# q and some softmax sums turned by VectorE in 32x32 blocks, in a fused attention and channel-mix kernel

## The chip, the cores and the metric

The kernel runs on one core of one Trainium2 chip. The core has engines that work side by side, each through its own instructions in order: TensorE (PE, with its weight loads as PEld), VectorE (DVE), ScalarE (ACT), GpSimd (POOL) and SyncE (SP); POOL and SP mostly issue DMAs here. The metric is the device time in microseconds of one execution; lower is better. A measured time is a median of several executions. A profile is one further execution with its own time.

## The reference

Inputs are fp32: q, k, v of shape 8 x 8 x 576 x 64 (batch, head, token, head dimension), phi of 8 x 8 x 576 x 32, and the weights of a channel mix. The work per batch and head is an attention with 32 memory slots in place of keys:

```python
a = phi - np.max(phi, axis=2, keepdims=True)
a = np.exp(a)
a = a / (np.sum(a, axis=2, keepdims=True) + 1e-09)      # over tokens
k_m = np.einsum('bhsm,bhsd->bhmd', a, k)
v_m = np.einsum('bhsm,bhsd->bhmd', a, v)
scores = scale * np.matmul(q, k_m.transpose(0, 1, 3, 2))
attn = np.exp(scores - np.max(scores, axis=-1, keepdims=True))
attn = attn / (np.sum(attn, axis=-1, keepdims=True) + 1e-09)   # over the 32 slots
x = np.matmul(attn, v_m)          # then heads side by side: 8 x 576 x 512
x_prev = x shifted by one token, zero at each batch's start
xk = mu_k * x + (1.0 - mu_k) * x_prev
xr = mu_r * x + (1.0 - mu_r) * x_prev
k = np.maximum(xk @ w_k, 0.0)     # 512 -> 1024
v = k * k @ w_v                   # 1024 -> 512
r = 1.0 / (1.0 + np.exp(-(xr @ w_r)))
out = r * v
```

Neither maximum is taken on the chip.

## The kernel before

**Layout.** A batch's 8 heads form HH = 4 pairs; g is the pair and c (0 or 1) the head in it. Where slots lie on partitions, pair g has the 32 partitions from 32 g on, for each c. q, k and v come in as bf16 with 128 partitions, where a partition holds a run of NJ = 9 tokens for each pair; rows 0 to 63 belong to c = 0, rows 64 to 127 to c = 1 (ROWS). A batch's tokens are worked in two column halves of 320 and 256 (HALVES).

**Steps of a batch.** PLAN (L18 to L38) is an order written out by hand: a list of words, run from left to right, each issuing a step's instructions to their engines. So it fixes the order on every engine and every queue. A word "3:l2" is step l2 of batch 3. The steps are: exp (exponential of phi, L225), z (sum over tokens as matmuls, and reciprocal, L247 to L250), kv or k, v (k_m and v_m, L237), nk and nv (scaled by the reciprocal, L274, L281), tk (k_m turned by TensorE and copied to kmT, L301 to L305), q0 and q1 (q turned), s0 and s1 (scores and their exponentials e, L358 to L362), l0 to l3 (denominators: a matmul with ones sums the 32 slots and spreads the sum, then a logarithm, L372 to L377), r0z and r1z (exponential of minus the logarithm, L382), w0 and w1 (e times that, at, L389), x0 and x1 (times v_m, to PSUM, copied by ScalarE, L288 to L401), dd (difference to the token before, L413), and k0d, k2d, r0d, r2d (the two mixes, L423 to L424, written to rings xk_T and xr_T). Batches 0 and 1 take a shorter way for the mixes: nk0 to nr1, y0 to y3 and mk0 to mr1 (mixed, L437) put mu into v_m and mix in PSUM. A suffix c, hn, ht, h0z or qh marks a step on half a batch.

**Steps of the channel mix.** "c3:5" is key step 5 of token chunk 3 (512 tokens; chunk 0 in two halves a and b): 4 matmuls, relu on ScalarE (rl, three buffers), square on VectorE (sq, L520 to L528). "g:7" is the gate of 128 tokens: 4 matmuls, exponential (L548), and for odd ones a logarithm and exponential over the pair (L550, L551). "o:7" is the value: 8 matmuls, a product with the gate on VectorE and the store (L565 to L567; L505 for the DMA on SP). "p:..." words and "load" issue loads on POOL's queue ("2:load" loads batch 4; LOADS, L40, gives the order phi, k, v, q, and k, q, v for batch 2). "0:busy4" puts four matmuls of zeros on TensorE. "0:mub" and "0:mu" prepare mu.

**How q is turned.** The scores need q with the head dimension on partitions. Batch 0 (qh0, qh1; L319) and batches 1 to 4 (q0, q1; L333) do it on TensorE: matmuls with the identity to PSUM, then copies by VectorE (and ScalarE for batches 0 and 1). Batches 5 to 7 (qx, L314) use a DMA that turns, issued from SP; "5:hold" (L263) is a tiny POOL copy that makes POOL's queue wait for batch 5's turned q before "5:load" overwrites q. Two tokens' 64 elements share one turned block of 128 rows, so that even and odd token runs j lie in different row halves; for that reason JT (L46) puts the nine runs in the order 0 2 4 6 8 1 3 5 7, and the store (L504) undoes it.

**Shared buffers.** All matmul outputs go through one pool of 8 PSUM banks, handed out in the order of PLAN; scores' two halves are matmuls on tiles of 64 rows x 32 columns of the array, written as

```python
for g in (0, 2, 1, 3):
    m = slice(g * M, (g + 1) * M)
    for hf in range(2):
        n = [NJ * g + j for j in JT[5 * hf:5 + 4 * hf]]
        r = ROWS[n[0] % 2]
        nc.tensor.matmul(pss[hf][m, :], lhsT=st["kmT"][r, c, m], ...)
```

Of the kernel before, what the change touches and what calls it, by code (L numbers as in the profile page):

```python
# [10 lines left out]
F32 = mybir.dt.float32  # L11
BF16 = mybir.dt.bfloat16
AF = mybir.ActivationFunctionType
# [5 lines left out]
    "p:q:0a 0:exp1 0:exp0 0:z 0:k0c p:q:0b 0:hn0 0:qh0 0:ht0 0:qh1 p:k:0b 0:s0 0:mub p:v:0a 0:l0 0:k1c 0:l1 0:hn1",  # L19
    "p:v:0b 0:mu 0:ht1 p:wr:0-4 0:h1z 0:v0c 0:s1 0:v1c p:phi:1 0:h0z 0:y1 0:l2 0:l3 0:nk0 0:y0 0:nk1 0:h3z 0:nr1",  # L20
    "p:wk:4-8 0:h2z 0:busy4 0:nr0 0:y3 0:y2 0:mr1 0:mr0 p:wk:0-4 0:mk1 1:exp g:2 g:0 0:mk0 g:3 1:z c0:2a c0:7b c0:6b",
    "c0:4a c0:1b p:k:1 p:q:1 c0:2b 1:k 1:nk c0:0b c0:7a c0:5b c0:3a c0:1a 1:q0 c0:3b 1:q1 1:tk c0:4b c0:0a 1:s0 p:v:1",
    "1:s1 1:v c0:6a 1:l1 1:nr1 1:l0 c0:5a p:wv:0-2 1:nk0 1:l2 p:wv:2-4 1:nk1 1:nr0 1:h1z 1:l3 0:load 1:y1 1:h2z 1:h0z",
    "1:h3z g:1 1:y3 o:3a o:2a 1:y2 1:y0 o:2b o:3b 1:mk1 o:1b 1:mk0 1:mr0 c1:5 1:mr1 c1:2 2:exp c1:6 c1:3 c1:1 c1:0",
    "1:load 2:z g:4 g:5 2:q1 2:q0 2:kv 2:nk o:0b 2:load o:1a 2:tk 3:exp 2:nv c1:7 2:s1 2:s0 c1:4 2:l2 o:0a 2:l1 3:z",
    "2:l0 2:r0z 2:w0 2:l3 2:r1z 2:w1 o:4 o:5 2:x0 3:kv 3:nk 3:nv g:6 3:tk 3:q0 3:q1 2:x1 2:dd 2:k0d g:7 g:8 3:s0",
    "2:k2d 3:s1 o:6 o:7 3:l0 2:r2d 3:l2 3:load 3:l1 2:r0d 3:l3 3:r1z c2:3 4:exp c2:2 c2:5 3:r0z 3:w1 c2:0 3:w0 c2:4",
    "c2:6 g:10 c2:1 4:z 3:x1 4:kv 4:nk 4:nv c2:7 3:x0 g:11 3:dd 4:q0 4:q1 4:tk 5:exp o:11 g:9 5:qx o:10 5:z 5:kv",
    "3:k0d 4:s1 3:k2d 4:s0 o:9 g:12 4:l3 5:nk 3:r0d 4:l2 c3:2 c3:6 5:nv 4:l0 4:l1 4:r1z 4:w1 c3:3 4:r0z 4:w0 5:tk",
    "c3:7 c3:4 3:r2d c3:0 c3:5 5:s0 5:hold 5:load 4:x1 o:8 c3:1 5:l1 4:x0 4:dd g:13 4:k2d 5:l0 g:14 o:13 4:load o:12",  # L30
# [14 lines left out]
NJ = 9  # L45
JT = (0, 2, 4, 6, 8, 1, 3, 5, 7)  # L46
# [3 lines left out]
def kernel(  # L50
# [23 lines left out]
    QR = S // NJ  # L74
    HALVES = (slice(0, 5 * QR), slice(5 * QR, S))
# [135 lines left out]
    def attention(b):  # L211
# [51 lines left out]
        def hold():  # L263

            spare = work.tile([1, 2], BF16, name="spare", tag="spare", bufs=1)
            nc.gpsimd.tensor_copy(spare, st["qT"][0:1, :, 0, 0])

        def norm_k(cs=(0, 1)):

            def go():  # L270
                if "kbd" not in st:
                    st["kbd"] = work.tile([128, 2, 2, D], BF16, name="kbd", tag="kbd", bufs=3)
                for c in cs:
                    nc.vector.tensor_scalar_mul(  # L274
                        st["kbd"][:, c], st["k"][c].unsqueeze(1).to_broadcast([128, 2, D]), st["rz"][:, c:c + 1])
            return go
# [30 lines left out]

        def q_tile():
            if "qT" not in st:
                st["qT"] = work.tile([128, 2, HH * NJ // 2, QR], BF16, name="qT", tag="qT", bufs=3)  # L310
            return st["qT"]

        def cross_q():
            for hg in range(2):  # L314
                nc.sync.dma_start_transpose(out=q_tile()[:, hg],
                                            in_=qs[b % 2][ROWS[hg]].rearrange("p n d -> p (n d)"))

        def tr_q_rows(hg):

            def go():  # L320
                r = ROWS[hg]
                for i in range(2):
                    ps = ps_tile([128, NJ, QR], BF16, "qtps")
                    for n in range(NJ):
                        n0 = 2 * (NJ * i + n)
                        nc.tensor.matmul(ps[:, n], rhs=identity[r, r], is_transpose=True,  # L326
                                         lhsT=qs[b % 2][r, n0:n0 + 2, :].rearrange("p n d -> p (n d)"),
                                         start=True, stop=True, skip_group_check=True)
                    (nc.scalar.copy if i else nc.vector.tensor_copy)(q_tile()[:, hg, NJ * i:NJ * (i + 1)], ps)
            return go  # L330

        def tr_q(i):
            def go():  # L333
                pss = [ps_tile([128, NJ, QR], BF16, "qtps") for _ in range(2)]
                for n in range(NJ):
                    n0 = 2 * (NJ * i + n)
                    for hg in range(2):
                        r = ROWS[hg]
                        nc.tensor.matmul(pss[hg][:, n], rhs=identity[r, r], is_transpose=True,  # L339
                                         lhsT=qs[b % 2][r, n0:n0 + 2, :].rearrange("p n d -> p (n d)"),  # L340
                                         start=True, stop=True, skip_group_check=True)
                for hg in range(2):
                    (nc.scalar.copy if b < 2 and hg else nc.vector.tensor_copy)(
                        q_tile()[:, hg, NJ * i:NJ * (i + 1)], pss[hg])
            return go

        def scores(c):

            def go():
                if "e" not in st:  # L350
                    st["e"] = work.tile([128, 2, S], BF16, name="e", tag="e", bufs=3)
                pss = [half_tile(hf, "scps") for hf in range(2)]
                for g in (0, 2, 1, 3):
                    m = slice(g * M, (g + 1) * M)
                    for hf in range(2):
                        n = [NJ * g + j for j in JT[5 * hf:5 + 4 * hf]]
                        r = ROWS[n[0] % 2]
                        nc.tensor.matmul(pss[hf][m, :], lhsT=st["kmT"][r, c, m],  # L358
                                         rhs=st["qT"][r, c, n[0] // 2:n[-1] // 2 + 1].rearrange("p j t -> p (j t)"),
                                         start=True, stop=True, skip_group_check=True)  # L360
                for hf in range(2):
                    nc.scalar.activation(st["e"][:, c, HALVES[hf]], pss[hf], AF.Exp, scale=scale)  # L362
            return go
# [20 lines left out]

        def weigh(c, sl=slice(0, S)):
# [51 lines left out]
        def mixed(w, hf):  # L437

            def go():
# [7 lines left out]
                for i in range(ND):  # L447
# [27 lines left out]
        for i in range(2):  # L475
            steps[f"s{i}"] = scores(i)
# [19 lines left out]
    def store(o, t, cols):  # L496
        g = t * 128
        eng = nc.sync
        while g < (t + 1) * 128:
# [4 lines left out]
            dst = out[b].rearrange("(p j) d -> p j d", j=NJ)[p0:p0 + n, JT[j], cols]  # L504
# [32 lines left out]
    def gate(t):  # L537

        def go():
# [5 lines left out]
            if t % 2 == 0:  # L545
# [3 lines left out]
            if t % 2 == 1:  # L549
# [71 lines left out]
```

## Time and profile before

| what | value |
|---|---|
| time, median of 3 runs | 208.34 us (207.24 to 208.76) |
| the profiled execution | 208.79 us, its span 207.0 us |
| TensorE busy | 192.7 us (93%) |
| VectorE busy | 133.9 us (65%) |
| ScalarE busy | 159.4 us (77%) |
| GpSimd busy | 29.6 us (14%) |
| mean TensorE clock granted | 0.998 |
| HBM read, written | 38.28 MB, 9.44 MB |

The span runs from the first to the last instruction; the execution's own time lies a little over it. Busy time of TensorE counts pipelined matmuls with modelled ends, so that rows of matmuls overlap, and where one block ends is read better from the start of the next. A row of the groups gives line, engine, operation, output and inputs with shapes, count, then busy time and mean ns of one, then the idle time before them and what ended it. A row of the view of waits reads: who waited, for whom, us in total, times, longest. Lengths of neighbouring VectorE rows overlap by some hundredths of a microsecond.

### The profile page before, as it was taken

Reading aid. Unit: us, or ns where it says so; the run is one execution under the profiler, and the core shown is the slowest. Engines: PE = TensorE matmul, PEld = TensorE weight load, DVE = VectorE, ACT = ScalarE, POOL = GpSimd, SP = SyncE. Lnnn points to the kernel's source line nnn. Section 1 sums busy time; section 2 is a strip of 40 time slices with the busy share of each in tenths; the row PEclk is TensorE's granted clock in tenths of the full one; section 3 lists DMA queues with packets and bytes.
Section 4 is the critical chain, followed back from the end, with each engine's and each line's share of the span. In section 5 each row is a group of like instructions: output and inputs, shape, how many; then the busy total and the mean of one; then the engine's idle time right before and its main releaser. Section 6 shows DMA issues by size and latency. Waiting matters only on the chain.

```text
span 207.0 us, 5511 instructions
## 1 busy us (share of the span) xinstructions
PE 192.7 (93%) x2213; PEld 103.6 (50%) x2235; DVE 133.9 (65%) x360; ACT 159.4 (77%) x314; POOL 29.6 (14%) x46
## 2 busy tenths in 40 slices
PE   0489999999999999999999999999999999999992
PEld 0355577745655445544458654444444444444441
DVE  1236455884668996899594969767887856615232
ACT  3246999987968998979899977899968655686570
POOL 7644222201504000007400000000000000000000
PEclk9999999999999999999999999999999999999999
DMA  6999999999999999298999997832060215202525
GB/s 160 178 208 260 207 207 205 261 221 292 209 284 240 262 269 201 61 133 205 187 231 298 198 165 115 189 71 52 0 152 5 51 33 119 54 0 62 135 67 141
DMA packets 31641, 33.06 MB, mean 160 GB/s; under 512 B 9072, under 2 KB 26752, under 8 KB 31616
## 3 DMA queue, kind: packets, MB, share of 16 engines
q0 software_dynamic: 17392, 20.91, 54.2%
q1 hardware_dynamic: 13456, 10.96, 24.5%
q10 hardware_dynamic: 768, 0.85, 1.3%
q8 instruction: 17, 0.28, 0.5%
q14 instruction: 8, 0.07, 0.1%
HBM read 38.28 MB, written 9.44 MB: 231 GB/s over the span
## 4 chain that ended last, share of the span: by engine, by line
PE 89%; DMA 6%; issue 1%; POOL 1%; ACT 1%; DVE 0%; SPq 0%; POOLq 0%; DVEq 0%
PE pk L520 31%; PE pv L565 29%; PE pr L543 15%; DMA q<-in_q_dram 4%; PE kvps L237 3%; PE zps L372 2%; PE mxps L288 2%; DMA qT<-q 2%; PE scps L358 2%; PE nops L288 2%; PE qtps L339 1%; PE idle L195 1%; PE zps L247 1%; PE mub L200 1%; PE qtps L326 1%
## 5 line engine op out<-in xcount | busy, mean ns | idle before, releaser
L520 PE MATMUL pk<-xkT,wk 128*128 128x512 bf16 (+4 forms) x346 | 66.9, 340 | 0.4
L565 PE MATMUL pv<-wv,sq 128*128 128x512 bf16 (+1 forms) x322 | 65.6, 353 | 0.4
L524 ACT ACTIVATE rl<-pk 128x512 bf16<-128x512 f32 (+3 forms) x80 | 41.9, 560 | 9.9 <-PE pk L520 8.7
L528 DVE TENSOR_TENSOR sq<-rl 128x512 bf16<-128x512 bf16 (+5 forms) x104 | 32.3, 340 | 26.0 <-ACT rl L524 25.0
L565 PEld LDWEIGHTS <-sq 128*128 128x128 bf16 x328 | 31.4, 98 | 30.0 <-issue 0.5
L520 PEld LDWEIGHTS <-wk 128*128 128x128 bf16 x352 | 32.9, 98 | 26.5 <-issue 0.5
L567 DVE TENSOR_TENSOR o<-sg,pv 128x512 f32<-128x512 f32 (+1 forms) x41 | 24.9, 619 | 18.9 <-PE pv L565 14.1
L543 PE MATMUL pr<-wr,xrT 128*128 128x512 bf16 x134 | 34.6, 381 | 0.5
L548 ACT ACTIVATE sg<-pr 128x512 f32<-128x512 f32 x36 | 21.3, 611 | 12.3 <-PE pr L543 5.2
L543 PEld LDWEIGHTS <-xrT 128*128 128x128 bf16 x144 | 13.5, 98 | 15.4 <-ACT xrT L449 0.4
L550 ACT ACTIVATE sg<-sg 128x1024 f32<-128x1024 f32 x18 | 19.0, 1057 | 0.6
L551 ACT ACTIVATE sg<-sg 128x1024 f32<-128x1024 f32 x18 | 19.0, 1057 | 0.6
L401 ACT CAST x<-nops 128x320 bf16<-128x320 f32 (+1 forms) x48 | 15.8, 428 | 3.6 <-PE nops L288 3.6
L423 DVE TENSOR_SCALAR mu_d<-diff,mu 128x576 bf16<-128x576 bf16 x48 | 15.5, 364 | 0.1
L389 DVE TENSOR_TENSOR atn<-e,lz 128x576 bf16<-128x576 bf16 (+2 forms) x20 | 12.4, 635 | 4.0 <-ACT lz L382 3.8
L377 ACT ACTIVATE lz<-zps 128x320 f32<-128x320 f32 (+1 forms) x32 | 11.9, 420 | 1.6 <-PE zps L372 1.6
L362 ACT ACTIVATE e<-scps 128x320 bf16<-128x320 f32 (+1 forms) x32 | 11.0, 416 | 1.5 <-PE scps L358 1.5
L382 ACT ACTIVATE lz<-lz 128x576 f32<-128x576 f32 (+2 forms) x20 | 11.6, 600 | 0.2
L413 DVE TENSOR_TENSOR diff<-x 128x1024 bf16<-128x1024 bf16 (+1 forms) x18 | 9.0, 554 | 3.4 <-ACT x L401 3.4
L225 ACT ACTIVATE em<-ph 128x1152 bf16<-128x1152 f32 (+1 forms) x9 | 9.4, 1050 | 2.1 <-DMA ph<-in_phi_dram 2.1
L237 PE MATMUL kvps<-kv,em 64*32 64x128 bf16 (+1 forms) x720 | 9.3, 219 | 1.0 <-DMA kv<-in_k_dram 1.0
L424 DVE TENSOR_TENSOR xkT<-x,mu_d 128x1152 bf16<-128x1152 bf16 x12 | 9.1, 759 | 0.4
(66 smaller groups left out, 140.7 us busy)
## 6 DMA issues: line engine op xcount, KB each, us to landing
out_dram<-o SPq DMA_DIRECT2D x61, 128.0 KB, 2.4
ph<-in_phi_dram POOLq DMA_DIRECT2D x7, 576.0 KB, 20.8
kv<-in_k_dram POOLq DMA_DIRECT2D x7, 576.0 KB, 17.3
q<-in_q_dram POOLq DMA_DIRECT2D x7, 576.0 KB, 21.3
kv<-in_v_dram POOLq DMA_DIRECT2D x7, 576.0 KB, 18.8
out_dram<-o SPq DMA_DIRECT2D x18, 64.0 KB, 5.6
wk<-in_moe_w_k_dram POOLq DMA_DIRECT2D x2, 512.0 KB, 14.7
wv<-in_moe_w_v_dram POOLq DMA_DIRECT2D x2, 512.0 KB, 20.0
```

Source lines behind the costliest of these rows:

```text
L237: nc.tensor.matmul(kvps[c][g * M:(g + 1) * M], lhsT=em[ROWS[c], j, g, :], rhs=kv5[ROWS[c], parts, g, j, :], start=j == 0, stop=j == NJ - 1 ...
L401: nc.scalar.copy(st["x"][:, i, sl], pss[i])
L423: nc.vector.tensor_scalar_mul(t[:, i], st["d"][:, pr + i, :], mu1[:, o:o + 1])
L520: nc.tensor.matmul(pk[:, p0 - lo:p1 - lo], lhsT=wk_sb[:, di, fi * 128:(fi + 1) * 128], rhs=xk_T[:, di, p0 % RING:p0 % RING + p1 - p0], sta ...
L524: nc.scalar.activation(rl, pk, AF.Relu)
L528: nc.vector.tensor_mul(sq[:, fi, p:p + p1 - p0], rl[:, p0 - lo:p1 - lo], rl[:, p0 - lo:p1 - lo])
L543: nc.tensor.matmul(pr, lhsT=xr_T[:, di, c0:c0 + 128], rhs=wr_sb[:, di, :], start=(di == 0), stop=(di == ND - 1))
L548: nc.scalar.activation(sg[:, t % 2], pr, AF.Exp, scale=-1.0)
L550: nc.scalar.activation(sg, sg, AF.Ln, bias=1.0)
L551: nc.scalar.activation(sg, sg, AF.Exp, scale=-1.0)
L565: nc.tensor.matmul(pv[:, cols], lhsT=sq[:, fi, p:p + 128], rhs=wv_sb[:, fi, cols], start=(fi == 0), stop=(fi == NF - 1))
L567: nc.vector.tensor_mul(o[:, cols], gated[t // 2][:, t % 2, cols], pv[:, cols])
```

## The change

q is turned by VectorE for all batches. VectorE's turn works on 32x32 blocks of 32-bit words; the bf16 data are read as words, so that a word holds two neighbouring elements of the head dimension and stays whole. The steps q0 and q1 now issue one VectorE instruction each (128 partitions, 576 words); qh0 and qh1 of batch 0 turn 64 partitions with 1152 words. TensorE's and the DMA's turning, their PSUM copies, JT, qx and hold go away. qT has two buffers in place of three.

After the turn a partition quadrant holds, for one c and one half of the token rows, 32 words of the head dimension, and the two elements of each word lie side by side (index h). So a score is the sum of two matmuls over 32 rows each (h = 0 and 1), with kmT split the same way (norm_k writes even and odd elements apart, and repeats them for the two token halves). Scores use tiles of 32 x 32, with the moving operand read at every second element; step "s" does both c of a batch at once in four PSUM banks, while batch 0 keeps s0 and s1. The exponentials write e with tokens in their natural order, and the differences, mixes and stores use that order.

For batches 5 to 7 the denominators no longer go through TensorE and ScalarE. "fe" turns e in 32x32 word blocks, "fs" sums over the 32 slots along the free axis and takes the reciprocal, and "fo" spreads that over 32 and turns it back into lz. These replace l0 to l3 and r0z, r1z there.

The gate's logarithm and second exponential are a step of their own ("sg:3" for the pair 3). PLAN is written anew, loads included: weights come as wk's lower half, wr, wk's upper half; batch 2 loads in the common order.

```diff
 PLAN = [
-    "p:q:0a 0:exp1 0:exp0 0:z 0:k0c p:q:0b 0:hn0 0:qh0 0:ht0 0:qh1 p:k:0b 0:s0 0:mub p:v:0a 0:l0 0:k1c 0:l1 0:hn1",
-    "p:v:0b 0:mu 0:ht1 p:wr:0-4 0:h1z 0:v0c 0:s1 0:v1c p:phi:1 0:h0z 0:y1 0:l2 0:l3 0:nk0 0:y0 0:nk1 0:h3z 0:nr1",
-    "p:wk:4-8 0:h2z 0:busy4 0:nr0 0:y3 0:y2 0:mr1 0:mr0 p:wk:0-4 0:mk1 1:exp g:2 g:0 0:mk0 g:3 1:z c0:2a c0:7b c0:6b",
-    "c0:4a c0:1b p:k:1 p:q:1 c0:2b 1:k 1:nk c0:0b c0:7a c0:5b c0:3a c0:1a 1:q0 c0:3b 1:q1 1:tk c0:4b c0:0a 1:s0 p:v:1",
-    "1:s1 1:v c0:6a 1:l1 1:nr1 1:l0 c0:5a p:wv:0-2 1:nk0 1:l2 p:wv:2-4 1:nk1 1:nr0 1:h1z 1:l3 0:load 1:y1 1:h2z 1:h0z",
-    "1:h3z g:1 1:y3 o:3a o:2a 1:y2 1:y0 o:2b o:3b 1:mk1 o:1b 1:mk0 1:mr0 c1:5 1:mr1 c1:2 2:exp c1:6 c1:3 c1:1 c1:0",
-    "1:load 2:z g:4 g:5 2:q1 2:q0 2:kv 2:nk o:0b 2:load o:1a 2:tk 3:exp 2:nv c1:7 2:s1 2:s0 c1:4 2:l2 o:0a 2:l1 3:z",
-    "2:l0 2:r0z 2:w0 2:l3 2:r1z 2:w1 o:4 o:5 2:x0 3:kv 3:nk 3:nv g:6 3:tk 3:q0 3:q1 2:x1 2:dd 2:k0d g:7 g:8 3:s0",
-    "2:k2d 3:s1 o:6 o:7 3:l0 2:r2d 3:l2 3:load 3:l1 2:r0d 3:l3 3:r1z c2:3 4:exp c2:2 c2:5 3:r0z 3:w1 c2:0 3:w0 c2:4",
-    "c2:6 g:10 c2:1 4:z 3:x1 4:kv 4:nk 4:nv c2:7 3:x0 g:11 3:dd 4:q0 4:q1 4:tk 5:exp o:11 g:9 5:qx o:10 5:z 5:kv",
-    "3:k0d 4:s1 3:k2d 4:s0 o:9 g:12 4:l3 5:nk 3:r0d 4:l2 c3:2 c3:6 5:nv 4:l0 4:l1 4:r1z 4:w1 c3:3 4:r0z 4:w0 5:tk",
-    "c3:7 c3:4 3:r2d c3:0 c3:5 5:s0 5:hold 5:load 4:x1 o:8 c3:1 5:l1 4:x0 4:dd g:13 4:k2d 5:l0 g:14 o:13 4:load o:12",
-    "7:exp 5:r0z 4:k0d g:16 5:w0 g:15 7:z 7:kv 5:s1 c4:5 7:qx c4:1 c4:4 6:qx 4:r0d 7:nv c4:0 c4:3 6:exp 5:l2 7:nk",
-    "5:l3 c4:6 c4:2 c4:7 5:r1z 5:w1 4:r2d g:17 o:15 o:16 7:tk 5:x0 o:17 6:z 5:x1 6:kv 6:nk 7:s0 6:nv g:18 6:tk 5:dd",
-    "5:k0d g:19 5:k2d o:18 o:14 6:s0 6:s1 c5:6 c5:0 6:l3 5:r0d 6:l2 6:l0 6:l1 c5:2 c5:5 6:r0z c5:7 c5:3 6:r1z 6:w1",
-    "7:l0 6:w0 c5:1 g:20 7:l1 c5:4 7:s1 6:x1 5:r2d o:19 7:r0z 6:x0 6:dd 6:k2d 7:l3 g:22 6:k0d 7:w0 g:21 7:l2 g:23",
-    "7:r1z o:20 o:21 7:w1 o:23 6:r2d c6:0 c6:6 c6:4 g:26 c6:1 c6:5 7:x1 c6:3 6:r0d c6:2 c6:7 7:x0 7:dd o:22 g:24 g:27",
-    "7:k2d 7:k0d g:25 o:25 o:26 7:r2d o:24 c7:5 g:30 c8:6 c7:0 c7:2 c7:1 c8:1 o:27 c8:4 c7:7 6:load 7:r0d c7:3 c7:6",
-    "c7:4 c8:2 c8:7 g:28 g:29 c8:3 c8:0 c8:5 g:31 o:28 o:29 o:31 7:load g:32 o:30 g:33 g:34 g:35 o:32 o:33 o:34 o:35",
+    "p:q:0a 0:exp1 0:exp0 0:z 0:k0c 0:mub 0:qh0 p:k:0b 0:k1c p:q:0b 0:hn1 0:hn0 p:v:0b 0:ht1 0:ht0 0:s0 0:qh1 0:s1",
+    "p:v:0a 0:l0 0:l1 0:l2 0:v1c 0:h1z p:wk:0-4 0:h2z 0:nr1 0:l3 0:v0c 0:y2 0:h0z 0:nk0 0:y0 0:h3z 0:y1 0:nk1",
+    "p:wr:0-4 p:wk:4-8 0:busy4 0:y3 0:nr0 0:mk1 0:mk0 p:phi:1 0:mr0 c0:1b c0:2b c0:0a c0:4a 0:mr1 p:k:1 p:q:1 c0:1a",
+    "1:exp c0:7b g:2 g:3 c0:4b p:v:1 p:wv:0-2 1:z 1:k sg:1 1:nk 1:q0 g:0 c0:7a c0:3a c0:6a c0:0b g:1 1:tk 1:q1 c0:2a",
+    "c0:5b c0:5a 1:s 1:v 1:nr1 1:nr0 c0:3b p:wv:2-4 1:nk0 1:l1 1:nk1 0:mu c0:6b 1:l2 1:h1z 1:l0 1:h2z 1:y1 1:y2 1:l3",
+    "1:h0z o:3a o:2a 1:y0 1:h3z o:2b 1:y3 sg:0 o:3b 1:mr0 1:mk0 g:5 0:load 1:mk1 g:4 2:exp c1:1 c1:6 c1:0 2:z 1:mr1",
+    "o:1b 2:kv 2:nk o:0b 2:tk 2:nv 2:q0 1:load sg:2 2:q1 c1:7 c1:2 c1:4 2:s c1:3 c1:5 3:exp 2:l2 2:l0 2:l3 o:5 2:l1",
+    "2:r0z 2:r1z 2:w0 3:z 2:w1 o:1a o:4 3:kv 3:nk 3:nv 2:x0 o:0a g:8 3:tk 3:q0 2:x1 3:q1 2:dd 2:k0d g:7 g:6 3:s",
+    "2:load 2:k2d sg:3 o:6 2:r0d 3:l1 o:7 3:l3 3:load 2:r2d 4:exp c2:4 3:l2 c2:6 3:l0 3:r0z c2:2 3:r1z 3:w1 4:z 3:w0",
+    "c2:7 c2:0 c2:3 g:9 4:kv 3:x1 4:nv 4:nk c2:1 c2:5 3:x0 5:exp 4:tk 4:q1 4:q0 g:10 3:dd sg:4 3:k0d g:11 o:9 4:s o:8",
+    "3:k2d 3:r0d sg:5 o:11 5:z 5:kv 4:l3 c3:2 4:l1 5:q1 g:12 5:nk 3:r2d 4:l2 c3:5 5:q0 4:l0 4:r1z c3:3 c3:0 5:load",
+    "4:r0z 4:w1 4:w0 g:13 c3:6 5:nv sg:6 5:tk 4:load c3:7 c3:4 c3:1 4:x1 o:10 7:q1 7:q0 4:x0 o:13 4:dd 7:exp o:12",
+    "4:k2d g:17 g:15 7:z 4:k0d 5:s 7:kv 5:fe 7:nk 6:exp g:14 g:16 5:fs c4:0 c4:5 4:r2d 7:nv 6:z 7:tk 5:fo sg:7 o:15",
+    "5:w1 sg:8 o:14 7:s 5:w0 c4:1 c4:6 c4:4 6:kv 4:r0d 5:x0 6:nk c4:2 c4:3 7:fe c4:7 6:q0 5:x1 g:19 5:dd 6:q1 o:16",
+    "o:17 g:21 6:tk 6:nv 5:k2d 5:k0d 7:fs g:18 sg:9 g:20 6:s o:18 6:fe c5:0 6:fs c5:2 c5:5 c5:3 6:fo c5:6 6:w0 6:w1",
+    "c5:1 c5:4 c5:7 5:r0d 5:r2d sg:10 o:19 6:x1 o:20 7:fo o:21 7:w0 g:23 6:x0 7:w1 6:load g:22 sg:11 6:dd o:22 g:24",
+    "g:25 6:k0d 7:x0 6:k2d o:23 7:x1 7:dd 6:r0d g:26 7:k0d c6:2 7:k2d 7:load c6:3 6:r2d c6:1 sg:12 c6:5 c6:7 7:r2d",
+    "c6:0 c6:6 c6:4 c7:1 c7:2 c7:7 c7:4 g:27 sg:13 c7:6 o:26 c7:5 7:r0d c7:0 o:25 o:24 g:29 c7:3 o:27 c8:5 c8:1 g:31",
+    "c8:0 g:30 c8:2 sg:15 g:28 sg:14 c8:7 c8:6 o:31 o:30 c8:4 g:32 g:33 o:28 c8:3 o:29 sg:16 g:35 g:34 sg:17 o:33",
+    "o:32 o:34 o:35",
 ]
-LOADS = {None: ("phi", "k", "v", "q"), 2: ("phi", "k", "q", "v")}
+LOADS = {None: ("phi", "k", "v", "q")}
-JT = (0, 2, 4, 6, 8, 1, 3, 5, 7)
+    PB = QR // 2
...
-        def hold():
-            spare = work.tile([1, 2], BF16, name="spare", tag="spare", bufs=1)
-            nc.gpsimd.tensor_copy(spare, st["qT"][0:1, :, 0, 0])
...
                     nc.vector.tensor_scalar_mul(
-                        st["kbd"][:, c], st["k"][c].unsqueeze(1).to_broadcast([128, 2, D]), st["rz"][:, c:c + 1])
+                        st["kbd"][:, :, c],
+                        st["k"][c].rearrange("m (d h) -> m h d", h=2).unsqueeze(2).to_broadcast([128, 2, 2, PB]),
+                        st["rz"][:, c:c + 1])
...
-        def cross_q():
...
-        def tr_q_rows(hg):
...
-        def tr_q(i):
...
+        def turn_q(rows_, gs):
+            def go():
+                dst = q_tile()[rows_, gs].rearrange("p g n h -> p (g n h)")
+                src = qs[b % 2][rows_, gs.start * NJ:gs.stop * NJ].rearrange("p n d -> p (n d)")
+                nc.vector.transpose(dst.bitcast(U32), src.bitcast(U32))
+            return go
-        def scores(c):
+        def scores(cs):
...
+                pss = {(c, hf): ps_tile([128, NJ, PB], F32, "scps") for c in cs for hf in range(2)}
+                for h in range(2):
+                    for g in range(HH):
+                        m = slice(g * M, (g + 1) * M)
+                        for c in cs:
+                            for hf in range(2):
+                                r = slice((2 * c + hf) * PB, (2 * c + hf + 1) * PB)
+                                nc.tensor.matmul(pss[c, hf][m].rearrange("p j t -> p (j t)"), lhsT=st["kmT"][r, h, m], rhs=st["qT"][r, g, :, h],
+                                                 start=h == 0, stop=h == 1, skip_group_check=True)
+                for c in cs:
+                    e = st["e"][:, c].rearrange("p (j w t) -> p w j t", w=2, t=PB)
                     for hf in range(2):
+                        nc.scalar.activation(e[:, hf], pss[c, hf], AF.Exp, scale=scale)
...
+        def fold_e():
+            eT = work.tile([128, 2 * NJ, M, 2], BF16, name="eT", tag="eT", bufs=1)
+            nc.vector.transpose(eT.rearrange("p b m h -> p (b m h)").bitcast(U32),
+                                st["e"].rearrange("p c s -> p (c s)").bitcast(U32))
+            st["eT"] = eT
+        def fold_sum():
+            st["se"] = work.tile([128, 2 * NJ, 2], F32, name="se", tag="se", bufs=2)
+            nc.vector.reduce_sum(st["se"], st["eT"].rearrange("p b m h -> p b h m"), axis=mybir.AxisListType.X)
+            nc.vector.reciprocal(st["se"], st["se"])
+        def fold_out():
...
+            nc.vector.transpose(st["lz"].rearrange("p c (b t h) -> p (c b) h t", t=PB, h=2),
+                                st["se"].unsqueeze(3).to_broadcast([128, 2 * NJ, 2, M]))
...
-        before = [[(QR, 5 * QR, 5 * QR), (1, QR, 4 * QR)], [(5 * QR, S, 0)]]
+        before = [[(QR, 5 * QR, 0), (1, QR, S - QR)], [(5 * QR, S, 4 * QR)]]
...
-            steps[f"q{i}"] = tr_q(i)
-            steps[f"qh{i}"] = tr_q_rows(i)
+            steps[f"q{i}"] = turn_q(slice(0, 128), slice(2 * i, 2 * i + 2))
+            steps[f"qh{i}"] = turn_q(ROWS[i], slice(0, HH))
...
-            dst = out[b].rearrange("(p j) d -> p j d", j=NJ)[p0:p0 + n, JT[j], cols]
+            dst = out[b].rearrange("(p j) d -> p j d", j=NJ)[p0:p0 + n, j, cols]
...
-            if t % 2 == 1:
-                nc.scalar.activation(sg, sg, AF.Ln, bias=1.0)
-                nc.scalar.activation(sg, sg, AF.Exp, scale=-1.0)
+    def settle(p):
+        def go():
+            nc.scalar.activation(gated[p], gated[p], AF.Ln, bias=1.0)
+            nc.scalar.activation(gated[p], gated[p], AF.Exp, scale=-1.0)
+        return go
```

## The prediction

> **What bounds the kernel now.** I read the page's busy shares and slices first, then what TensorE waited for, then the chain that ended last, then single rows. The page:
>
> ```profile
> span 207.0 us, 5511 instructions
> PE 192.7 (93%) x2213; PEld 103.6 (50%) x2235; DVE 133.9 (65%) x360; ACT 159.4 (77%) x314; POOL 29.6 (14%) x46
> PE   0489999999999999999999999999999999999992
> PEclk9999999999999999999999999999999999999999
> ```
>
> TensorE is full from the fourth slice to the last but one, at full clock. All that it waited for, by the view of waits:
>
> ```profile
> PE zps L247 <- ACT em L225: 5.9, 1, 5.9
> PE qtps L326 <- DMA q<-in_q_dram: 1.6, 2, 0.8
> PE kvps L237 <- DMA kv<-in_k_dram: 1.0, 1, 1.0
> PE scps L358 <- DMA qT<-q: 0.4, 1, 0.4
> PE zps L372 <- ACT e L362: 0.2, 1, 0.2
> ```
>
> 8.5 us of this fall before 12 us; behind that only 0.6. So from about 20 us on, time is TensorE work, and an edit pays by the TensorE time it removes, as long as no new wait arises. Pieces of the chain (start, length, what):
>
> ```profile
> 31.22 0.37 PE qtps L339 x18
> ...
> 32.13 0.37 PE qtps L339 x18
> ...
> 50.86 0.63 PE qtps L339 x36
> ...
> 132.26 0.49 PE zps L372 x4
> ```
>
> Rows of groups:
>
> ```profile
> L389 DVE TENSOR_TENSOR atn<-e,lz 128x576 bf16<-128x576 bf16 x12 | 9.0, 756 | 2.4 <-ACT lz L382 2.2
> L389 DVE TENSOR_TENSOR atn<-e,lz 128x320 bf16<-128x320 bf16 x4 | 1.9, 487 | 0.9 <-ACT lz L382 0.9
> L343 DVE COPY qT<-qtps 128x576 bf16<-128x576 bf16 x14 | 5.5, 450 | 1.3 <-PE qtps L339 1.2
> ```
>
> And TensorE's timeline (start, length to the modelled end):
>
> ```profile
> 123.06 0.80 PE L237 MATMUL kvps<-kv,em 64*32 64x128 bf16 x72
> 123.65 0.35 PE L358 MATMUL scps<-qT,kmT 64*32 64x320 bf16 x8
> 138.97 0.33 PE L358 MATMUL scps<-qT,kmT 64*32 64x320 bf16 x8
> 139.23 0.32 PE L288 MATMUL nops<-atn,vb 32*64 32x256 bf16 x8
> ```
>
> **What leaves TensorE.** (1) q's turning, batches 1 to 4: 0.37 + 0.37 + 3 x 0.63 = 2.6 us. Batches 5 to 7 were turned by DMA and cost TensorE only their 0.4 us wait; that goes too. (2) Denominators of batches 5 to 7: four matmuls are 0.49, so 1.5 us. (3) Batch 0's two turnings (1.14 us each) end at 12.1 us, in a stage that waits for loads and pads with 1.7 us of idle matmuls, so removing them brings little by itself.
>
> **Scores.** Now two blocks of 8 matmuls per batch; 138.97 to 139.23 is 0.26 for a block, 0.52 per batch. New: 32 matmuls on 32x32 tiles, two rounds of 16 with 288 columns. The Trainium skill (TensorE: Matmul & The Clock Gate, "Wait — 56ns, not 53.3ns?") says that starts are never under about 25 ns apart; by it 32 take 0.8 us plus some 0.1 of entry, 0.4 a batch more than now, and the change loses 3.2 us on eight batches. The trace speaks against using this for matmuls on different tiles: 72 of kvps take 0.59 us from their first start to the next block's (0.73 in the chain), 8 to 10 ns each. I take the row: a ninth of it, a round of 8 with 128 columns, is 0.065 us, so a round of 288 takes 0.14, two 0.28, and about 0.12 for entering and leaving a tiling, which is what a block of 0.26 has over its 320 columns: 0.4 us. Gain 0.1 on seven batches, loss 0.2 on batch 0, whose two blocks stay apart: +0.5 us. Bounds: -3.2 and +1.0. That the moving operand now takes every second element no row shows; I price it at nothing, and the lower bound covers it.
>
> **Start.** Batch 0's q halves are turned by VectorE, 1.36 us each, after they land (8.7 us; the second, now behind a k half, about 12.4). Mixing needs v, whose second half lands at 5.0 + 10.3 = 15.3; then v's 0.65, and 2 us of VectorE rows to the last weight: about 18.0 against 19.2 now. But the weights are reordered: upper wk comes third; from 17.8 (where the first weight block lands now: issue 5.55, 12.2 to landing) at 2.5 us per block, as wk's two are apart (21.7, 24.2), it lands near 22.8. The fourth key step (c0:4a) needs it; TensorE would be there at 21.3 (three mixes and three key steps behind 18.0) and waits 1.5. At 22.8 it then has 1.9 us less done than now at 24.9 (three gates at 0.864, a mix at 0.5 and z at 0.2 are left, 1.4 of key steps done), so the start gains 0.2 us. Bounds -1.0 and +1.1.
>
> Sum: 2.6 + 0.4 + 1.5 + 0.5 + 0.2 = 5.2 us, if no wait is added.
>
> **VectorE.** No row shows a turn or a reduction. The nearest is L389, one pass from SBUF at one element a cycle: (756 - 487) / 256 = 1.05 ns per element, 151 fixed. A half of q is 576 words of 32 bits: 0.76 us, 0.68 start to start since rows overlap by 0.08; 1152 words 1.36 (1.28). Lower end 0.38 (two words a cycle, as L424's 1152 bf16 in 0.76), upper end 1.3 (two cycles a word). The Trainium skill (VectorE: DVE Perf Modes, "The three transpose paths") gives 311 ns for 128 columns of bf16, 178 over one per cycle, so 0.78 for a half: 0.02 off, nothing in the sum. Added: q 14 x 0.68 + 2 x 1.28 = 12.1; per batch of 5 to 7 0.68 for e, 1.28 for the reduction, 0.12 reciprocal, 1.28 for the spread, 3.4; three are 10.1. Removed: 16 PSUM copies, 0.37 each start to start (four take 1.46), 5.9. Net +16, 134 to 150 us of about 203. ScalarE loses 4 x 0.64 in copies and per late batch four logarithms (1.68) and two exponentials (1.39): -11.8, to 148. Permuted access in kbd, e's writes and the output rows keep their sizes: nothing, bounds +-0.5. Splitting the gate's second half into steps moves ScalarE work to places where it has more room than now.
>
> The average hides the tight place. Between batch 6's tk and r2d the new order has on TensorE 7 gates of 0.864, 6 values of 1.73, 10 key steps of 0.864, four x of 0.27, s and tk: 26.8 us. On VectorE: 10 mixes of 1.355 (13.6), two reductions and reciprocals (2.8), one turn of e (0.7), two spreads (2.6), four weighings (2.7), two differences (3.2), 6 products (3.6), 10 squares (3.8), tk and nv 0.6: 33.6 us. It ends this stage some 6.8 us late. Today's steepest place, from 5:r2d to 7:w0, has 7.2 us of VectorE beside 3.0 of TensorE, and TensorE waits for nothing. Cover: 8 PSUM banks, three rl buffers, and the late items (7's mixes) are first needed by c7. I let it cost 0.5 us; without the cover it costs the whole 6.8. Just before, from 5:s on, the same count ends 0.4 us late, so the stage begins level.
>
> **Queues.** SP loses six turning DMAs and keeps the stores. POOL loses the hold, which kept it waiting 28.1 us (to 93.5); batch 7's k, v and q can then go at about 84.5 to 87, after batch 5's k, v, q are used, so loads end earlier. But turning now waits for q inside VectorE's order, where squares and output products stand behind it. Where it lands is the issue's start and the last column of the DMA view; batch 5's q, issued at 64.65, by that view:
>
> ```profile
> q<-in_q_dram POOLq DMA_DIRECT2D x1, 576.0 KB, 20.7
> ```
>
> So it lands at 85.4, batch 3's at 38.4 + 22.4 = 60.8; batch 2's last load, which q becomes, at about 49 (27.64 + 21). The new order reaches these turns at about 48, 61 and 86, and batch 7's at 96: from c0:4a at 22.8, the TensorE steps written before each, at the lengths above, sum to 25.4, 38.1, 63.4 and 73.6 us. Batch 7's q (three loads at 3.4 us each behind phi, from 87) lands near 97. Each is within a microsecond; TensorE has 2.6 us of key steps before 2:s and more elsewhere. I take 0.5 us in all.
>
> New waits 1.0, net 4.2. The profiled execution took 208.79 with a span of 207.0, 1.8 around it; span 202.8, execution 204.6. The median of the runs (208.34) lies 0.45 below the profiled one: **204.1**, which I write as 204.0.
>
> **Rivals.**
> (A) Loads: q lands later than I count, or the upper wk does; VectorE stops for 2 us at three places and half reaches TensorE: 3 us of waits in place of 1: 206.0. For it: DMA engines are busy in nine tenths up to 83 us. Against: the counts agree so closely.
> (B) VectorE becomes the bound late, its rows as I cost them: 6.8 us late, buffers cover half, and chains through ScalarE (scores, exponentials, turn of e) add 0.3: 3.7 us in place of 0.5: 207.2, no difference. For it: four stages in a row go through the two engines. Against: today's 33.25 busy of 38 us (62 to 100) without a wait.
> (C) Slower: a 32-bit turn takes two cycles a word. Then a 576-word unit costs 0.6 more; six units before the tight stage and five in it add 6.6 us, 13.4 late at its end; less some 6 of cover is 7.4 of waits in place of 0.5: 211.0. It decides from about 0.4 us more per unit (1.1 us for half a q), where 4.4 us of lag eat the gain. For it: the trace has no 32-bit row at this; against: L389 reads fp32 beside bf16 at one a cycle.
> (D) The removed work was not on the path: excluded by TensorE's full slices, but for batch 0.
>
> **Chances.** Forecast 0.60, A 0.12, B 0.14, C 0.14. Over 1% faster means under 206.3, about what a measurement can tell: the forecast and most of A, 0.70; within 1% 0.16; slower 0.14. Range 201.6 (start gains 1.1, no waits, scores +1.0) to 208.8 (over B, short of C).
>
> **What would show it.** Right: no qtps group; a DVE turn of 128x576 near 0.76 us and 128x1152 near 1.36; s near 0.4 us; TensorE's waits after 25 us under 2 us; VectorE near 150 us. Wrong: TensorE waiting for DVE rl or x chains between about 120 and 150 us (B, C), VectorE waiting for q's DMA more than 3 us (A), or s near 0.9.

## The result, and the profile after

The changed kernel takes 205.66 us (median of 4 runs, 204.93 to 206.27) against 208.12 us for the kernel before beside it (4 runs, 207.24 to 208.76). The ratio is 0.9884, with a 95% interval of 0.9858 to 0.9910: 1.2% faster, 2.5 us. I had forecast 204.0, 4.3 us less. The sign holds, and so does the range (201.6 to 208.8, wide enough to hold no gain too), but 1.8 us of the gain is missing. Three executions of the kernels below, 208.68 to 210.41 us long at a slightly lower clock, are slow ones and are left out of every number here.

The page of the changed kernel (its profiled execution took 205.91 us, 1.8 of that around the span):

```profile
span 204.1 us, 5371 instructions
PE 187.7 (92%) x2152; PEld 98.4 (48%) x2173; DVE 147.5 (72%) x372; ACT 148.5 (73%) x292; POOL 29.4 (14%) x45
PE   0469999999999999999979999999999999999992
DVE  1266747848578997997499999999999948404332
PEclk9999999999999999999999999999999999999998
PE 72%; DVE 14%; DMA 7%; ACT 3%; issue 2%; DVEq 0%; POOLq 0%
```

TensorE is full as before, but for one slice near 102 us. VectorE, with 13.6 us more work, is now full from there to 163 us. Of the chain that ended last, VectorE holds 14%; in the kernel before it held less than 1%:

```profile
PE 89%; DMA 6%; issue 1%; POOL 1%; ACT 1%; DVE 0%; SPq 0%; POOLq 0%; DVEq 0%
```

This share is rough: in experiment 6, whose late part is the same, it is 7%.

What TensorE waited for, by the view of waits:

```profile
PE zps L249 <- ACT em L227: 6.3, 1, 6.3
PE kvps L239 <- DMA kv<-in_k_dram: 1.8, 2, 1.1
PE kvps L239 <- DVE o L565: 1.0, 1, 1.0
PE scps L333 <- DVE qT L318: 0.7, 1, 0.7
PE scps L333 <- DVE kmT L305: 0.6, 2, 0.4
PE ktps L300 <- DVE kbd L271: 0.6, 1, 0.6
```

Behind 25 us there is one wait of weight, kvps for an output product of VectorE, 1.0 us. The groups of the new operations:

```profile
L318 DVE STREAM_TRANSPOSE qT<-q 128x576 uint32<-128x576 uint32 x14 | 10.4, 761 | 2.8 <-DMA q<-in_q_dram 2.8
...
L375 DVE STREAM_TRANSPOSE lz<-se 128x1152 f32<-128x1152 f32 x3 | 4.1, 1372 | 0.0
...
L369 DVE TENSOR_REDUCE se<-eT 128x36 f32<-128x1152 bf16 x3 | 4.0, 1343 | 0.0
...
L318 DVE STREAM_TRANSPOSE qT<-q 64x1152 uint32<-64x1152 uint32 x2 | 2.7, 1368 | 0.0
...
L363 DVE STREAM_TRANSPOSE eT<-e 128x576 uint32<-128x576 uint32 x3 | 2.3, 770 | 0.0
...
L370 DVE RECIPROCAL se<-se 128x36 f32<-128x36 f32 x3 | 1.1, 378 | 0.1
```

A turn is (1372 - 761) / 576 = 1.06 ns per 32-bit word, whatever the word holds, and the 64-partition form gives 1.05; the sizes are those that the prediction took from L389.

**Where the time went.** I cut TensorE's time from batch 1's z to its last matmul into blocks, each from its start to the next one's, in both profiles. Before, the stretch runs from 24.7 to 203.2 us, after from 27.4 to 200.4. The changed kernel reaches that mark 2.7 us later, but with 2.5 us more work done (seven half key steps, 3.35 us, where the old order had one gate, 0.86).

| term, us gained | predicted | measured |
|---|---|---|
| q's turning, batches 1 to 4 | 2.6 | 2.6 |
| denominators, batches 5 to 7 | 1.5 | 1.5 |
| scores, batches 1 to 7 | 0.7 | 0.2 |
| start, with batch 0's scores | 0.0 | -0.2 |
| waits, net of the 0.4 that goes | -0.6 | -1.3 |
| sum | 4.2 | 2.8 |

The spans differ by 2.9. So what leaves TensorE was counted right; scores and waits were not. The start's term is no surer than half a microsecond: kernels with the same start reach batch 1's z between 26.5 and 27.4 us, and this profile is the latest of them.

**The scores.** A piece of the changed kernel's chain (start, length, what):

```profile
33.98 0.41 PE scps L333 x23
```

And TensorE's timeline in the kernel before, at batch 2's two blocks:

```profile
54.98 0.46 PE L358 MATMUL scps<-qT,kmT 64*32 64x320 bf16 x16
55.38 1.04 PE L520 MATMUL pk<-xkT,wk 128*128 128x512 bf16 x4
```

A batch's block lasts 0.40 to 0.43 us, and the forecast was 0.4. The mistake is on the other side. In the kernel before, the blocks of batches 5 and 7 stand apart and take 0.26 to 0.28 each, as I had read; but of batches 2 to 4 the two follow each other and take 0.40 to 0.48 together. The mean is 0.45 a batch, not 0.52.

**The wait of 1.0 us.** POOL's timeline of the changed kernel (start, length, then idle before and what ended it), at the loads of batch 7:

```profile
87.51 0.74 POOL L109 DMA_DIRECT2D kv<-in_k_dram  x1 [15.33 <-PE zps L348]
...
93.18 0.74 POOL L109 DMA_DIRECT2D q<-in_q_dram  x1 [4.18 <-DVE sq L522]
```

VectorE's timeline:

```profile
89.25 0.77 DVE L318 STREAM_TRANSPOSE qT<-q 128x576 uint32<-128x576 uint32 x1
...
92.11 0.77 DVE L318 STREAM_TRANSPOSE qT<-q 128x576 uint32<-128x576 uint32 x1
...
101.61 1.44 DVE L318 STREAM_TRANSPOSE qT<-q 128x576 uint32<-128x576 uint32 x2 [2.31 <-DMA q<-in_q_dram]
102.97 0.65 DVE L565 TENSOR_TENSOR o<-sg,pv 128x512 f32<-128x512 f32 x1
103.55 1.48 DVE L406 TENSOR_TENSOR diff<-x 128x1024 bf16<-128x1024 bf16 x3
...
105.02 0.68 DVE L565 TENSOR_TENSOR o<-sg,pv 128x512 f32<-128x512 f32 x1
```

TensorE's:

```profile
88.19 1.03 PE L537 MATMUL pr<-wr,xrT 128*128 128x512 bf16 x4
...
90.05 0.30 PE L348 MATMUL zps<-e,sumh 128*128 128x320 bf16 x1
...
104.27 0.49 PE L333 MATMUL scps<-qT,kmT 32*32 32x288 bf16 x32
105.75 0.80 PE L239 MATMUL kvps<-kv,em 64*32 64x128 bf16 x72 [0.99 <-DVE o L565]
```

k and v went at 87.5 as I had counted, but q waits until batch 5's q has been turned, whose second half VectorE reaches only at 92.1. (The row names the square right behind the turn; in experiment 3's profile the same row names the turn.) It goes at 93.2, lands 8.4 us later and stops VectorE for 2.3 us. Behind the turn stand a product, a difference and a second product. By the order of PLAN the second one, o:12, frees the PSUM bank that batch 7's k and v take, eight outputs later in a pool of eight; it ends at 105.7, and TensorE goes on at 105.75.

The kernel of experiment 3 has the same steps up to here. In its profile q happened to land 1.4 us earlier, and this wait is gone; VectorE's and TensorE's timelines:

```profile
100.18 1.44 DVE L318 STREAM_TRANSPOSE qT<-q 128x576 uint32<-128x576 uint32 x2 [1.05 <-DMA q<-in_q_dram]
```

```profile
104.52 0.95 PE L239 MATMUL kvps<-kv,em 64*32 64x128 bf16 x72
```

### The profile page after: what moved, and what is told of

It reads as the page before. It is cut to its first block, busy times and chain, and to the rows that moved or that the text cites. A ratio compares the mean times of both kernels' runs of the same rounds, so it can differ in the third digit from the quotient of the medians.

```text
span 204.1 us, 5371 instructions
## 1 busy us (share of the span) xinstructions
PE 187.7 (92%) x2152; PEld 98.4 (48%) x2173; DVE 147.5 (72%) x372; ACT 148.5 (73%) x292; POOL 29.4 (14%) x45
## 4 chain that ended last, share of the span: by engine, by line
PE 72%; DVE 14%; DMA 7%; ACT 3%; issue 2%; DVEq 0%; POOLq 0%
PE pk L514 24%; PE pv L563 24%; PE pr L537 13%; DMA q<-in_q_dram 4%; PE kvps L239 3%; DMA kv<-in_k_dram 3%; DVE qT L318 2%; DVE sq L522 2%; PE scps L333 2%; PE mxps L287 2%; DVE se L369 1%; PE nops L287 1%; DVE mu_d L416 1%; PE zps L348 1%; DVE o L565 1%
## 5 line engine op out<-in xcount | busy, mean ns | idle before, releaser
L514 PE MATMUL pk<-xkT,wk 128*128 128x512 bf16 (+4 forms) x346 | 67.7, 341 | 0.3
L518 ACT ACTIVATE rl<-pk 128x512 bf16<-128x512 f32 (+3 forms) x80 | 42.4, 556 | 13.1 <-PE pk L514 7.9
L522 DVE TENSOR_TENSOR sq<-rl 128x512 bf16<-128x512 bf16 (+5 forms) x104 | 31.4, 336 | 24.3 <-ACT rl L518 23.4
L338 ACT ACTIVATE e<-scps 128x288 bf16<-128x288 f32 x32 | 10.6, 417 | 7.9 <-PE scps L333 7.9
L318 DVE STREAM_TRANSPOSE qT<-q 128x576 uint32<-128x576 uint32 (+1 forms) x16 | 13.1, 837 | 2.8 <-DMA q<-in_q_dram 2.8
L239 PEld LDWEIGHTS <-em 64*32 64x32 bf16 x720 | 7.6, 96 | 6.2 <-issue 6.2
L417 DVE TENSOR_TENSOR xrT<-x,mu_d 128x1152 bf16<-128x1152 bf16 x12 | 9.1, 759 | 0.4
```

What stands on the lines that cost most here:

```text
L239: nc.tensor.matmul(kvps[c][g * M:(g + 1) * M], lhsT=em[ROWS[c], j, g, :], rhs=kv5[ROWS[c], parts, g, j, :], start=j == 0, stop=j == NJ - 1 ...
L417: nc.vector.tensor_add(dst, st["x"][:, pr:pr + n], t)
L514: nc.tensor.matmul(pk[:, p0 - lo:p1 - lo], lhsT=wk_sb[:, di, fi * 128:(fi + 1) * 128], rhs=xk_T[:, di, p0 % RING:p0 % RING + p1 - p0], sta ...
L518: nc.scalar.activation(rl, pk, AF.Relu)
L522: nc.vector.tensor_mul(sq[:, fi, p:p + p1 - p0], rl[:, p0 - lo:p1 - lo], rl[:, p0 - lo:p1 - lo])
```

## The experiments

Each kernel ran beside the kernel before; ratios are to that, and with the changed kernel's 0.9884 they give the differences in us. Since single profiles reach batch 1's z up to 0.9 us apart, two spans are not compared closer than a microsecond; stretches within them are steadier, as experiment 2 shows.

**1. Does TensorE still set the time where VectorE is full?** Twelve matmuls of zeros more, 2.6 us, once in the stage in which VectorE is full and once late.

```diff
-    "... 6:fe c5:0 ..."
+    "... 6:fe 6:busy12 c5:0 ..."
```

> The changed kernel with 12 matmuls of zeros (12 x 0.216 = 2.6 us of TensorE, no other engine) just before c5:0, in the stage in which VectorE is busy without a gap. If TensorE still sets the time: +2.6 us, 208.2 us, level with the kernel before. If VectorE sets it by now: TensorE has spare time there and the time stays at 205.7 to 206.2.

Measured: 208.27 us, ratio 1.0007 (0.9987 to 1.0027), 2.6 us more than the changed kernel, give or take 0.7.

```diff
-    "... sg:13 c7:6 ..."
+    "... sg:13 7:busy12 c7:6 ..."
```

> The same 12 matmuls of zeros just before c7:6, where VectorE has room. Both theories: +2.6 us, 208.3 us. It shows the price of TensorE work at a place where nothing is disputed.

Measured: 207.95 us, ratio 1.0002 (0.9982 to 1.0022), 2.5 us more, give or take 0.7. In both places TensorE's work costs its full length, so TensorE is still on the path where VectorE is full. Whether VectorE is on it too is the next question.

**2. How much of VectorE's work is still covered?** The turn of e is issued twice for batches 5 to 7; the second repeats the first, 2.1 us in all by start to start.

```diff
-    "... 5:fe 7:nk ..."
+    "... 5:fe 5:fe 7:nk ..."
```

> The changed kernel with the turn of e done twice for batches 5 to 7: 3 x 0.69 = 2.1 us more of VectorE in the stage where it is full. If TensorE sets the time and buffers cover VectorE's lateness: 205.7 to 206.4. If VectorE sets it: +2.1, 207.8.

Measured: 207.47 us (205.93 to 208.73), ratio 0.9968 (0.9941 to 0.9994): 1.75 us more, give or take 0.8. Most of the added work shows, and the runs leave open whether all of it does. The view of busy time by stretches (stretch, its length, then PE, PEld, DVE, ACT, POOL busy with instructions, TensorE clock, DMA share, GB/s), of the changed kernel:

```profile
105.00:115.00 10.00, 8.99 (x159) 5.36 (x160) 9.86 (x27) 9.03 (x15) 0.00 (x0) 1.00 0.82 166
115.00:130.00 15.00, 14.89 (x203) 8.59 (x203) 14.90 (x40) 10.30 (x23) 0.00 (x0) 1.00 0.32 72
130.00:140.00 10.00, 9.95 (x54) 4.41 (x53) 9.93 (x19) 8.29 (x16) 0.00 (x0) 1.00 0.11 27
140.00:150.00 10.00, 9.95 (x59) 4.26 (x60) 9.73 (x20) 7.26 (x17) 0.00 (x0) 1.00 0.35 81
150.00:163.00 13.00, 12.95 (x67) 5.76 (x67) 12.80 (x35) 9.06 (x18) 0.00 (x0) 1.00 0.18 40
```

In the changed kernel VectorE is busy for 57.2 of these 58 us and TensorE for 56.7: the two are level, and TensorE hardly waits. With 2.1 us more on VectorE, TensorE has new waits in its view of waits:

```profile
PE scps L333 <- ACT sg L549: 0.7, 1, 0.7
...
PE nops L287 <- DVE atn L382: 0.4, 1, 0.4
...
PE pk L514 <- DVE xkT L417: 0.3, 1, 0.3
```

What they come to is read from two gates in TensorE's timeline, g:14 behind batch 7's k and v, ahead of the first doubled turn, and g:24 late in the stage. In the changed kernel:

```profile
106.48 1.90 PE L537 MATMUL pr<-wr,xrT 128*128 128x512 bf16 x7
...
146.79 1.89 PE L537 MATMUL pr<-wr,xrT 128*128 128x512 bf16 x8
```

With the doubled turn:

```profile
106.39 1.90 PE L537 MATMUL pr<-wr,xrT 128*128 128x512 bf16 x7
...
148.77 1.89 PE L537 MATMUL pr<-wr,xrT 128*128 128x512 bf16 x8
```

The stretch takes 40.31 us in the one and 42.38 in the other: 2.1 us more, all of the added work. (On to the key steps at 151.84 us it is 45.36; the kernels with the late zeros and of experiment 6, which change nothing in this stretch, take 45.36 too, and the one with 2.6 us of zeros in it 47.95.) So in this stage TensorE and VectorE hand work to each other on one path, and the work of each costs its length. The cover that I had let carry 6.8 us of VectorE's lateness exists, and the change uses it up.

**3. The new order without the denominators on VectorE.** For batches 5 to 7 the matmul with ones, the logarithm and the exponentials come back in the places of the three fold steps.

```diff
-    "... 5:fe ... 5:fs ... 5:fo ..."
+    "... 5:l0 5:l1 ... 5:l2 5:l3 ... 5:r0z 5:r1z ..."
```

> The changed kernel in its own order, with the denominators of batches 5 to 7 back on TensorE and ScalarE (l0, l1 in place of fe, l2, l3 of fs, r0z, r1z of fo). TensorE has 1.5 us more, ScalarE 9 more, VectorE 10.5 less. If TensorE sets the time: +1.5, 207.2 (206.5 to 207.5). If VectorE sets it: faster than 205, near 203.

Measured: 208.16 us (206.98 to 209.26), ratio 1.0008 (0.9980 to 1.0036). That is 2.6 us slower than the changed kernel, give or take 0.8, and level with the kernel before. Both forecasts missed: it is slower than 207.5, and nowhere near 203. The profiled execution, among the shorter ones with 207.69 us, shows what the four matmuls per batch bring beside their length: waits for ScalarE's exponentials of the scores, here in the view of waits,

```profile
PE zps L348 <- ACT e L338: 1.2, 3, 0.8
```

and the longest of them in TensorE's timeline:

```profile
131.80 0.41 PE L348 MATMUL zps<-e,sumh 128*128 128x320 bf16 x2 [0.84 <-ACT e L338]
```

One of the three, 0.2 us, falls in the start and stands in the changed kernel too; the other two are new and make 1.0. From batch 5's scores (104.10 us here, 104.27 in the changed kernel) to the key steps at 153.60 and 151.84 us this kernel takes 1.9 us more: 1.4 of matmuls, those 1.0, and half a microsecond in smaller pieces, less the wait of 1.0 for the output product, which it doesn't have. So the profile places 1.9 of the 2.6 us; the rest is within the interval. From 105 to 163 us ScalarE was the tighter of the two helpers in the kernel before (49.7 busy, VectorE 45.3). Here the sums' steps stand at places chosen for the fold steps; an order written for them might do better, so this run doesn't price q's turn in the best order for it.

**4. The old order with q turned by VectorE.** The old PLAN and loads, the turns in the places of q0, q1 and qx, no hold, scores one head of each pair at a time, denominators as before.

```diff
-    "... g:9 5:qx o:10 ... 5:s0 5:hold 5:load ..."
+    "... g:9 sg:4 5:q0 5:q1 o:10 ... 5:s0 5:load ..."
```

> The order of before, with q turned by VectorE at the places where TensorE or the DMA turned it, the loads' order of before, and the denominators on TensorE and ScalarE throughout. Theory that the removed TensorE work is the gain: it removes 2.6 of turning, 0.7 of scores, the 0.4 of waiting for the DMA, and may add a microsecond of waits for turns that stand too late: 204.5 to 206. Theory that the new order is the gain: 208 or more.

Measured: 209.26 us (208.31 to 210.15), ratio 1.0051 (1.0029 to 1.0073): 1.1 us slower than before, though 2.6 us of matmuls and a wait of 0.4 are gone. The profiled execution is its longest, 210.15 us. From its view of waits:

```profile
PE scps L334 <- DVE kmT L306: 2.1, 2, 1.1
PE pv L564 <- DVE sq L523: 0.5, 1, 0.5
...
PE pv L564 <- DVE o L566: 0.4, 1, 0.4
```

Of the first, 1.1 us stand in TensorE's timeline at batch 1's scores, where the kernel before has no wait:

```profile
34.88 0.51 PE L334 MATMUL scps<-qT,kmT 32*32 32x288 bf16 x32 [1.08 <-DVE kmT L306]
```

VectorE's timeline shows why: the copy of kmT stands behind the two turns, which were DMA or TensorE work when the order was written.

```profile
33.01 0.77 DVE L319 STREAM_TRANSPOSE qT<-q 128x576 uint32<-128x576 uint32 x1
...
33.88 0.77 DVE L319 STREAM_TRANSPOSE qT<-q 128x576 uint32<-128x576 uint32 x1
34.57 0.25 DVE L306 COPY kmT<-ktps 128x256 bf16<-128x256 bf16 x1
```

These three waits make 2.0 us (1.08 + 0.54 + 0.35). Scores take 0.6 more over seven batches, above all where a batch's two blocks stand apart and each of the new ones takes 0.38. From batch 1's z to the last matmul the profile is 0.4 us longer than before (178.9 against 178.5): 3.0 won, 2.6 lost, and some 0.8 lost in pieces too small to place. Batch 1's z itself comes 1.04 later (25.75 against 24.71), but there the first matmul waited 7.2 us for phi's exponential in place of 5.9, ahead of every changed step, so that part may be chance. The run shows that the removed TensorE work alone is no gain; where all of its 1.1 us go stays open.

**5. Batch 7's q in a buffer of its own.** A third q buffer lets its load go with k and v; kbd and kmT get two buffers in place of three to make room.

```diff
+    def q_rows(b):
+        return qs[2 if b == 7 else b % 2]
```

> The changed kernel with a third buffer for batch 7's q, so that its load needn't wait until batch 5's q is turned (92.9 us); it can be issued at about 89 in place of 93.2 and lands near 97.5 in place of 101.6. Two small pools get two buffers in place of three to make room. If batch 7's q is what cost TensorE its 1.0 to 1.2 us of waits between 100 and 115 us: 204.5. If those waits come from elsewhere: 205.7.

Measured: 205.80 us (205.29 to 207.34), ratio 0.9895 (0.9861 to 0.9929): no gain. The profiled execution is its longest, 207.34 us. POOL's and VectorE's timelines:

```profile
88.21 0.76 POOL L112 DMA_DIRECT2D q<-in_q_dram  x1
```

```profile
101.73 1.44 DVE L321 STREAM_TRANSPOSE qT<-q 128x576 uint32<-128x576 uint32 x2 [3.20 <-DMA q<-in_q_dram]
```

The load is issued 5.0 us earlier and q is turned at the same moment, not near 97.5; TensorE's wait for the output product stays, 1.6 us here. Batch 6's four loads, held behind it before, now follow at 88.9 to 91.2. That they take the DMA engines from it is the likely reason, but no run held them back, so it is not shown. As q came no earlier, this run doesn't tell what its lateness costs. Batch 7's q ahead of k and v in its own buffer wasn't tried.

**6. The start.** "0:mub", two slow matmuls of fp32 and their copy, is put behind batch 0's scores, so that VectorE reaches q's first half earlier.

```diff
-    "... 0:k0c 0:mub 0:qh0 ... 0:qh1 0:s1"
+    "... 0:k0c 0:qh0 ... 0:qh1 0:s1 0:mub"
```

> The changed kernel with the preparation of mu (mub: 1.2 us of TensorE, 0.8 of VectorE) moved from before batch 0's first turn of q to behind its second scores. The first turn starts at about 9.0 in place of 9.9. If the turns on VectorE hold the start: 0.4 to 0.8 us faster, 205.0. If v's landing and the chain behind it hold it: no change, 205.7.

Measured: 205.57 us (204.42 to 206.17), ratio 0.9864 (0.9829 to 0.9898). Against the changed kernel that is 0.4 us less, give or take 0.9, so it stays open. The first turn starts at 8.4 in place of 9.9 us, but TensorE's timeline shows what holds the scores' step before it, k's second half:

```profile
10.02 0.67 PE L239 MATMUL kvps<-kv,em 64*32 64x64 bf16 x36 [2.29 <-DMA kv<-in_k_dram]
```

The second scores start only 0.4 us earlier (13.67 against 14.07), and the moved matmuls, 1.2 us, now stand behind them and ahead of the denominators: the mixing starts at 19.6 us, in the changed kernel at 19.3.

**7. Five and six together.**

> Both of the last two edits. If both waits are on TensorE's path they add up: 204.0. If neither is: 205.7.

Measured: 206.12 us (204.29 to 206.76), ratio 0.9886 (0.9847 to 0.9925): nothing gained.

No kernel was clearly faster than the changed one. The old operations in the new order weren't tried, so what the order alone is worth is not separated from what it makes possible.

## Why the prediction was right or wrong

**What bounds the kernel: right, but not the whole of it.** TensorE's work costs its full length in the changed kernel (experiment 1), and rival D is out; for the kernel before it rests on TensorE's few waits. From 105 us on VectorE's work costs its length as well (experiment 2), and experiment 4 shows that TensorE's time can be removed without a gain.

**What leaves TensorE: right as lengths,** 2.6 and 1.5 us; as gains only in their sum. In the same order the sums on VectorE are worth 2.6 us, give or take 0.8 (1.9 in the profile), since waits of 1.0 for ScalarE go with them; this I had not seen. It is as much as the whole measured gain: the turned q with the new order but without the sums (experiment 3) is level with the kernel before, between 0.4 us faster and 0.7 slower. That the forecast came as near as it did is in part luck, as one share was worth more than counted and the other less.

**The turns: right.** A word takes 1.05 to 1.06 ns, as L389's element did, so rival C is excluded. VectorE's 147.5 and ScalarE's 148.5 stand against 150 and 148. The reciprocal is 0.38 us in place of 0.12; the row of two columns (164 ns) gives 6.3 ns for each further column, and I had costed it at L389's rate. That is 0.8 us of VectorE.

**Scores: the mechanism right, a term mis-sized.** "0.26 for a block, 0.52 per batch" took the length of a lone block for a pair. The gain is 0.2 in place of 0.7 us. The 25 ns between starts from the Trainium skill (TensorE: Matmul & The Clock Gate, "Wait — 56ns, not 53.3ns?") would have made the block 0.9 us; 32 matmuls on separate tiles take 0.41, 13 ns each, so the row was the better guide.

**Waits: mis-sized, 1.3 net in place of 0.6.** The failed step is the one on queues: "Batch 7's q (three loads at 3.4 us each behind phi, from 87) lands near 97. Each is within a microsecond". I summed TensorE's steps to find when VectorE reaches batch 5's turn, 86, and took it for one moment. TensorE is at the steps behind its two halves (g:12 and l0 of batch 4) at 88.2 and 90.1, and VectorE, running behind TensorE, starts the halves at 89.25 and 92.1. So q's load went at 93.2, 4.2 us later than right behind v's, q landed at 101.6, and 1.0 us of VectorE's 2.3 us of waiting came through; where q came 1.4 us earlier, it didn't (experiment 3's profile). This is rival A's mechanism, at one place in place of three. An earlier issue alone does not bring q earlier (experiment 5).

**Start: nearly right in sum, wrong in its parts.** Mixing began at 19.3, not 18.0, and no wait for the upper wk appears. I had counted from v's landing at 15.3, but v's halves stand in TensorE's order behind batch 0's second scores and its denominators. These scores wait 0.7 us for the second turn, start at 14.1, and v's halves run at 15.9 and 16.9. Net -0.2 where 0.0 was counted.

**The tight stage: half right.** "I let it cost 0.5 us; without the cover it costs the whole 6.8" holds in that TensorE is idle for only 0.1 us in 115 to 130 and about as little from 130 to 163. But I placed the risk in one stage, and VectorE is full from 105 us on, with no cover left: in experiment 2 all of 2.1 us shows in TensorE's timeline. Rival B's waits of 3.7 us did not come, but the changed kernel stands at their edge.

## What to carry to other kernels

Work moved off the bounding engine need not pay in an order written for the old engines: here q's turn in the old order lost 1.1 us, in part as a short copy that TensorE needed stood behind the new instructions. When an engine is nearly as full as the one that bounds, add up its own steps, not the bound's, to find when it reaches a step that releases a transfer. Where two engines that feed each other are both full, the work of each costs its length. A removed step can be worth more than its length, by the wait that its input had, so look at who feeds it and how full that one is.

## What the runs showed of the hardware

A VectorE turn costs 1.05 to 1.06 ns per 32-bit word, on 64 partitions as on 128, so bf16 data read as words moves two elements in that time; a source spread by broadcast costs the same (1372 ns for 1152 words on 128 partitions, 1368 without it on 64). A load issued 5.0 us earlier on POOL's queue came to use no earlier when others followed it at once (experiment 5; the reason is not shown). Two blocks of eight matmuls on different tiles took 0.40 to 0.48 us where they follow each other, and 0.26 to 0.28 each where they stand apart.
